# Hash attention and a SwiGLU block on one core: which thirds of x are transposed by DMA, and where one load, one cast of values and one eviction stand

## The chip, the core and the metric

The kernel runs on one core of a Trainium2 chip. Its engines run in parallel, each through its own queue in order: TensorE (PE in the profile; its weight loads are PEld), VectorE (DVE), ScalarE (ACT), GpSimd (POOL) and SyncE (SP), which here only issues DMAs. An instruction that waits holds up everything behind it on the same queue. Time is device microseconds of the core, the median of several runs; lower is better.

## The reference

```python
B, H, S, D = 4, 8, 768, 64                      # d_model = 512, d_ff = 1536
q_bits = (einsum("bhsd,dk->bhsk", q, proj) > 0)  # 6 bits: a bucket per row
k_bits = (einsum("bhsd,dk->bhsk", k, proj) > 0)
mask = q_bucket[..., :, None] == k_bucket[..., None, :]
scores = where(mask, q @ k.T / 8, -1e9)
attn = exp(scores - max); attn = attn / (sum(attn) + 1e-9)
x = (attn @ v), heads side by side               # 3072 x 512
xn = x / sqrt(mean(x * x) + 1e-6) * rms_g
g = xn @ w_gate; silu = g / (1 + exp(-g))
out = (silu * (xn @ w_val)) @ w_out              # 3072 x 512
```

All inputs and the output are float32; the kernel multiplies in fp16 and accumulates in float32.

## The kernel before, in words

**Units.** The work is cut into eight units u of 384 query rows: batch u // 2, half u % 2. For a unit and a head, the scores (transposed, keys on the partitions) come in three chunks of two 128 x 384 matmuls (`scores`, s_ps, L345). The hash bits are extra rows of the stationary and the moving operand, so that a wrong bucket makes the score very negative. ScalarE exponentiates a chunk (`probs`, psb, L357), and TensorE multiplies with the values (`av`, o_ps, L370, 18 matmuls a head), a column of ones giving the sum.

**From heads to x.** Two heads share the one bank of o_ps. VectorE evicts it (`attn_out`: otmp at L384, rcp at L389), which frees the bank for the next pair, and GpSimd multiplies (x at L391, its square sq at L397). `s_step` reduces sq to partial sums of squares (L413). After the last head `norm_scale` (ss at L435, rstd at L439) and `norm` scale the three thirds c of x, 128 rows each, into xn.

**Turning x.** The block needs x with features on the partitions (xnT). There are two ways. `turn_x` makes four 128 x 128 transposes on TensorE (x_ps, L463) and evicts them, on VectorE with one instruction (L469) or on ScalarE with four (L467), multiplying by the gains, a column per block (gcol). `turn_dma` (L427) issues one DMA transpose for the whole third from SyncE; then the gains, as rows (grow), are multiplied in already by the scaling (`scalar_tensor_tensor`, L448). The dictionary ONDMA says how many thirds of a unit go by DMA.

**The block.** For each of 12 slices of 128 hidden features there are four gate and four value matmuls (g_ps, v_ps, L480), a tanh on ScalarE (t, L488) and two instructions on VectorE (a at L497, ht at L498). `project` multiplies with w_out (y_ps, L509), and `store` copies (ysb, L521) and issues the DMA out (L522).

**The order.** It is written out by hand in 192 steps, three per head and unit (two of the first unit and two of the second go first). A step issues the scores of the next chunk, the exponentials of its own, and then whatever `plan[step]` holds, filled by `at(window, step, function)`. Unit u's block runs in the 24 steps in which unit u + 1 attends (NS = 24): `norm` at step 4 of them, the DMA transposes at step 5, and by `spread` the projection of unit u - 1, the turns on TensorE and the gates, given out evenly over the steps by weights (SCORES, AV, PROJ, FEED, TURN). For a third by DMA a piece of weight TURN without work is kept, except in unit 6. Steps in the list `late` (o_step, s_step, hash and its sends) are appended behind the pieces of `spread`, so that on VectorE an eviction stands behind the a and ht of the same step; the exceptions are named in the loop over `order`.

**Pairs of batches 1 to 3.** The table `spots` gives for a pair of heads (b, hp) the step of its load (eight DMAs of 32 x 24 x 32 and one of the values, `load_blocks` and `load_v`), of its transposes on VectorE (`turn_dve`), and of its hash (`hash_one`; the signs, L225, give the bits). `send_bits` issues four DMAs a head from SyncE into the operand; SENDS delays some. `zero_rows` (a memset of 2.65 us on GpSimd) clears the rows behind the bits. `v_prep` casts the values and `v_sum` adds them on GpSimd.

**The end.** After the last head, the projection of unit 6 runs by thirds, with `norm(7)` and the turns of unit 7 in it; then come unit 7's gates and its projection.

The PSUM banks of x_ps, g_ps, v_ps, y_ps and the like are three, used in turn; s_ps has two buffers, xnT two, xn one, ysb three. A DMA from SyncE waits for the one eight issues before it.

Of the kernel before, what the change touches and what calls it, by code (L numbers as in the profile page):

```python
# [19 lines left out]
DMODEL = H * D  # L20
DFF = 1536
NF = DFF // 128
# [11 lines left out]
def kernel(  # L34
# [12 lines left out]
    nc = tc.nc  # L47
# [27 lines left out]
    grow = const.tile([128, DMODEL], FP32, name="grow")  # L75
# [8 lines left out]
    def bank(name, shape=None, dt=FP32):  # L84
        return gps.tile(shape or [128, 512], dt, name=name, tag="g")
# [326 lines left out]
    def sumsq(u, hp, sq):  # L412
        nc.vector.tensor_reduce(  # L413
            out=ssp[u % 2][:, hp, :], in_=sq, op=ALU.add, axis=AX.X
        )
# [3 lines left out]

    rstds = {}  # L420

    ONDMA = {2: 2, 3: 2, 4: 2, 5: 2, 6: 3}

    def turn_dma(u, c):
        if c == 0:
            xnT[u] = npool.tile([128, 4, HALF], FP16, name="xnT", bufs=2)
        nc.sync.dma_start_transpose(  # L427
            out=xnT[u][:, :, c * 128 : (c + 1) * 128], in_=xn[u][:, c, :]
        )


    def norm_scale(u):

        ss = spool.tile([128, 3], FP32, name="ss")
        nc.vector.tensor_reduce(  # L435
            out=ss, in_=ssp[u % 2].rearrange("p h c -> p c h"), op=ALU.add, axis=AX.X
        )
        rstd = spool.tile([128, 3], FP32, name="rstd")
        nc.gpsimd.tensor_tensor(out=rstd, in0=ss, in1=mhalf, op=ALU.pow)  # L439
        rstds[u] = rstd  # L440

    def norm(u):
        if u not in rstds:
            norm_scale(u)
        xn[u] = npool.tile([128, 3, DMODEL], FP16, name="xn")
        for c in range(3 if u else 2):
            if c < ONDMA.get(u, 0):
                nc.vector.scalar_tensor_tensor(  # L448
                    out=xn[u][:, c, :], in0=x[u][:, c, :], scalar=rstds[u][:, c : c + 1],
                    in1=grow, op0=ALU.mult, op1=ALU.mult,  # L450
                )
            else:
                norm_third(u, c, nc.vector.tensor_scalar_mul)

    def norm_third(u, c, mul):
        mul(xn[u][:, c, :], x[u][:, c, :], rstds[u][:, c : c + 1])

    def turn_x(u, c, act=False):
        if c == 0:
            xnT[u] = npool.tile([128, 4, HALF], FP16, name="xnT", bufs=2)  # L460
        ps = bank("x_ps", [128, 4, 128], FP16)
        for kt in range(4):
            nc.tensor.transpose(ps[:, kt, :], xn[u][:, c, kt * 128 : (kt + 1) * 128], ident16)  # L463
        dst = xnT[u][:, :, c * 128 : (c + 1) * 128]
        if act:
            for kt in range(4):
                nc.scalar.mul(dst[:, kt], ps[:, kt], gcol[:, kt : kt + 1])  # L467
        else:
            nc.vector.tensor_mul(dst, ps, gcol.unsqueeze(2).to_broadcast([128, 4, 128]))  # L469
# [34 lines left out]
    def project(u, c, f0, f1):  # L504
        if f0 == 0:
            obank[u, c] = bank("y_ps")
        y = obank[u, c]
        for ft in range(f0, f1):
            nc.tensor.matmul(  # L509
                y, ht[u][:, ft, c * 128 : (c + 1) * 128], wo[:, ft, :],  # L510
                start=(ft == 0), stop=(ft == NF - 1),
            )

    def rows_of(u, c):
        b, half = divmod(u, 2)
        rows = out[b * S : (b + 1) * S, :].rearrange("(p c) n -> p c n", c=6)
        return rows[:, 2 * c + half if b in PARITY else 3 * half + c, :]

    def store(u, c):
        ysb = spool.tile([128, DMODEL], FP32, name="ysb", bufs=3)  # L520
        nc.scalar.copy(ysb, obank.pop((u, c)))  # L521
        nc.sync.dma_start(out=rows_of(u, c), in_=ysb)  # L522
# [65 lines left out]
    NS = 24  # L588
# [5 lines left out]
    def at(w, s, f, *a):  # L594
        plan[NS * w + s].append(lambda: f(*a))
# [70 lines left out]
    at(0, 1, load_natural, nc.sync, 0, 3, "q")  # L666
    at(0, 2, load_v, nc.sync, 0, 2)
    at(0, 2, load_v, nc.sync, 0, 3)
    at(0, 60, nc.sync.dma_start, grow, moe_rms_g.partition_broadcast(128))
    at(0, 65, nc.scalar.mul, grow, grow, float(DMODEL) ** 0.5)  # L670
    at(0, 6, v_prep, 0, 1)
    at(0, 15, v_prep, 0, 2)
    at(0, 19, v_prep, 0, 3, nc.vector)
# [9 lines left out]
    for hp, ts in ((0, (8, 22, 23, 24, 25, 24, 39, 26, 28, 42)), (1, (20, 27, 28, 29, 30, 29, 41, 32, 33, 43))):  # L683
# [15 lines left out]
    spots = {  # L699
        (1, 2): (34, (48, 48), (46, 46), 51),  # L700
        (1, 3): (45, (55, 56), (57, 58), 61),
        (2, 0): (50, (63, 64, 65, 66), (67, 69, 70, 71), 73),
        (2, 1): (62, (72, 73, 75, 81), (82, 83, 84, 85), 86),
        (2, 2): (70, (87, 88, 89, 90), (91, 93, 94, 95), 97),
        (2, 3): (84, (96, 97, 99, 105), (105, 106, 106, 107), 108),
# [2 lines left out]
        (3, 2): (114, (135, 136, 137, 139), (140, 141, 142, 143), 145),  # L708
        (3, 3): (132, (144, 145, 147, 153), (153, 154, 154, 155), 156),
    }  # L710
    for i, t in ((0, 39), (1, 41), (2, 57), (3, 61)):
        at(0, t, zero_rows, i)
    TX = 37

# [6 lines left out]
    def s_step(u, hp):  # L721
# [3 lines left out]
        else:  # L725
            sumsq(u, hp, sq)

    late = []
    for n, (u, h) in enumerate(order):
        t = 3 * n + 4 - ((u, h) == (0, H - 1))  # L730
        for part in range(2):
            at(0, t + part, av, u, h, part)
        if h % 2:
            if (u, h) == (0, H - 1):

                at(0, t + 1, o_step, u, h // 2, nc.vector)
                at(0, t + 1, norm_scale, u)
                at(0, t + 1, nc.vector.tensor_scalar_mul, gcol, gcol, float(DMODEL) ** 0.5)
                at(0, t + 2, hash_only, 1, 1)
                at(0, t + 2, hash_signs, 1, 1)  # L740
                at(0, t + 2, norm, u)
                at(0, TX-1, norm_third, u, 2, nc.scalar.mul)
                at(0, TX + 1, send_pair, 1, 1)
                for c in range(3):
                    at(0, TX, turn_x, u, c, c == 2)
                continue
            if (u, h) == order[-1]:
                at(0, t + 1, o_step, u, h // 2, nc.vector)
                continue

            steps = [(t + 1, o_step), (t + (6 if h < 7 else 3), s_step)]
            for s, step in steps:
                if s < 2 * NS or s % NS in (2, 4):
                    at(0, s, step, u, h // 2)
                else:
                    late.append((s, step, u, h // 2))
# [20 lines left out]
            inserts[2 * b * NS + s] = (MEAN, v_mean, b, hp, 4)  # L777


    SENDS = {(2, 0, 0): 77, (2, 0, 1): 77, (2, 2, 1): 101, (3, 2, 1): 149}  # L780

    def place(t, step):
        at(0, t, *step)
        if step[0] is hash_one:
            late.append((t, hash_bits, *step[1:]))
            for hh in range(2):
                s = SENDS.get((*step[1:], hh), t)
                late.append((max(s, t), send_bits, *step[1:], hh))
# [26 lines left out]
    for u in range(7):  # L815
        gates = [
            (FEED, f is gate and part == 0, [(0, f, u, ft, part)])
            for ft in range(NF) for f in (gate, value) for part in range(2)
        ]
        if u == 0:  # L820
            t0 = TX + 1
            spread(t0, 2 * NS - t0, gates)
            continue
        t0 = NS * (u + 1)
        at(0, t0 + 4, norm, u)
        for c in range(ONDMA.get(u, 0)):
            at(0, t0 + 5, turn_dma, u, c)
        pieces = []
        for i in range(9):
            c, n = divmod(i, 3)  # L830
            steps = [(0, project, u - 1, c, 4 * n, 4 * n + 4)]
            if n == 2:
                steps.append((1, store, u - 1, c))
            pieces.append((4 * PROJ, True, steps))
            if i in (6, 7):
                thirds = ((0,), (1, 2))[i - 6]
                for c in thirds:
                    if c >= ONDMA.get(u, 0):
                        pieces.append((TURN, False, [(0, turn_x, u, c)]))
                    elif u < 6:  # L840
                        pieces.append((TURN, False, []))
        lag, after = LAGS[u - 1 : u + 1]
        spread(t0 + lag, NS + after - lag, pieces + gates)
# [6 lines left out]
    def behind_norm(t):  # L850

        return t - t % NS + 9 if 1 <= t % NS < 9 else t

    for (b, hp), (load, kturns, qturns, _) in spots.items():
        at(0, load, load_blocks, nc.sync, b, hp)
        at(0, load, load_v, nc.sync, b, hp)
        at(0, min(kturns + qturns), new_pair, b, hp)
        for w, turns in (("k", kturns), ("q", qturns)):
            for i, t in enumerate(turns):
                at(0, t, turn_dve, b, hp, w, i, len(turns))  # L860
            t = turns[-1] + 1
            at(0, t if (b, hp) == (1, 2) else behind_norm(t), cast_pool, b, hp, w)
        t = 54 if (b, hp) == (1, 2) else behind_norm(qturns[-1] + 2)
        at(0, t, v_prep, b, hp)
        at(0, t, v_sum, b, hp)

# [13 lines left out]
    for t in range(LAST, LAST + 6):  # L880
        for f in plan[t]:
            f()
    for c in range(2):
        project(6, c, 0, NF)
        store(6, c)
    norm(7)
    project(6, 2, 0, 4)
    for c, f0, f1 in ((0, 4, 6), (1, 6, 8), (2, 8, NF)):
        turn_x(7, c, c == 1)
        project(6, 2, f0, f1)  # L890
    store(6, 2)
    for ft in range(NF):
# [37 lines left out]
```

## Time and profile before

| | |
|---|---|
| time, median of 3 runs | 328.9 us (328.4 to 329.17) |
| the profiled execution's own time | 328.83 us |
| its span | 326.7 us, 7791 instructions |
| granted TensorE clock | 1.000 |
| unit 1's first gate (g_ps) | at 79.27 us |
| unit 6's first gate | at 268.16 us |
| unit 7's first gate | at 300.08 us |
| DMA transposes (L427) | 11, SyncE busy 1.20 to 2.01 us in each |
| transposes on TensorE (L463) | 52 |

The table is to be read against TensorE's timeline: a gate of a unit is the first instruction that needs the whole of xnT, so its start shows whether the turning of x came in time. Times are from the span's start.

### The profile page before, as it was taken

The numbers are of one execution on the slowest core, as the hardware profiler recorded it, in microseconds if no ns is written. First come the engines' busy times: TensorE is split into PE (matmuls) and PEld (weight loads), VectorE is DVE, ScalarE is ACT, GpSimd is POOL, SyncE is SP. The second block draws the span as 40 slices with busy tenths as digits, with TensorE's granted clock in tenths as the row PEclk, the third lists the DMA queues.
The fourth block names the chain that finished last, engine by engine and source line by source line (L and its number), as shares of the span: only waits on it lengthen the run. The fifth ranks groups of instructions, "written<-read, shape, count | busy, mean of one in ns | idle before, by whom it ended". The sixth has DMA issues, their size and how long they took to land.

```text
span 326.7 us, 7791 instructions
## 1 busy us (share of the span) xinstructions
PE 321.3 (98%) x2955; PEld 194.1 (59%) x2955; DVE 231.2 (71%) x515; ACT 228.3 (70%) x332; POOL 157.6 (48%) x204
## 2 busy tenths in 40 slices
PE   8999999999999999999999999999999999999996
PEld 3576666656565565655566565655666556665554
DVE  5887876859888559874888568885766536675870
ACT  6999887667688667776777677787777767744322
POOL 3999759955974363731873521752682220221000
PEclk9999999999999999999999999999999999999999
DMA  7952999989328828343547047002100040002002
GB/s 216 353 163 69 230 216 200 181 138 182 102 39 155 152 79 154 54 98 99 91 102 141 9 138 135 7 1 69 68 5 3 7 127 14 2 2 90 8 2 96
DMA packets 85741, 32.63 MB, mean 100 GB/s; under 512 B 70908, under 2 KB 82632, under 8 KB 85704
## 3 DMA queue, kind: packets, MB, share of 16 engines
q1 hardware_dynamic: 81800, 27.35, 36.1%
q0 software_dynamic: 3680, 4.72, 8.6%
q8 instruction: 23, 0.38, 0.5%
q14 instruction: 14, 0.11, 0.1%
q10 hardware_dynamic: 224, 0.07, 0.1%
HBM read 28.58 MB, written 6.29 MB: 107 GB/s over the span
## 4 chain that ended last, share of the span: by engine, by line
PE 95%; DMA 2%; ACT 1%; SPq 1%; issue 0%
PE s_ps L345 20%; PE g_ps L480 19%; PE v_ps L480 19%; PE y_ps L509 17%; PE o_ps L370 11%; PE d_ps L216 2%; PE t_ps L156 2%; PE d_ps L236 2%; DMA qn<-in_q_dram 1%; PE x_ps L463 1%; ACT psb L357 1%; PE y_ps L528 1%; DMA xnT<-xn 1%; PE m_ps L329 1%; PE z_ps L576 1%; SPq L427 0%
## 5 line engine op out<-in xcount | busy, mean ns | idle before, releaser
L357 ACT ACTIVATE psb<-s_ps,ebias 128x768 f16<-128x768 f32 x192 | 168.1, 901 | 21.2 <-PE s_ps L345 20.4
L345 PE MATMUL s_ps<-QK 128*128 128x384 f16 (+1 forms) x384 | 93.5, 326 | 1.3 <-ACT psb L357 1.1
L488 ACT ACTIVATE t<-g_ps 128x384 f32<-128x384 f32 x96 | 47.3, 492 | 51.9 <-PE g_ps L480 50.2
L480 PE MATMUL g_ps<-xnT,wg 128*128 128x384 f16 x384 | 82.5, 326 | 0.2 <-DMA xnT<-xn 0.2
L480 PE MATMUL v_ps<-xnT,wv 128*128 128x384 f16 x384 | 81.8, 326 | 0.0
L497 DVE SCALAR_TENSOR_TENSOR a<-t,g_ps 128x384 f32<-128x384 f32 x96 | 53.0, 552 | 28.8 <-ACT t L488 27.3
L391 POOL TENSOR_TENSOR x<-otmp,rcp 128x384 f32<-128x384 f32 x30 | 25.1, 837 | 97.8 <-DVE rcp L389 97.6
L509 PE MATMUL y_ps<-wo,ht 128*128 128x512 f16 x276 | 67.9, 379 | 0.0
L498 DVE SCALAR_TENSOR_TENSOR ht<-a,v_ps 128x384 f16<-128x384 f32 x96 | 53.2, 554 | 12.1 <-PE v_ps L480 4.1
L370 PEld LDWEIGHTS <-psb 128*128 128x128 f16 x1152 | 51.8, 97 | 16.1 <-issue 1.2
L370 PE MATMUL o_ps<-vl,psb 128*128 128x65 f16 x1152 | 55.8, 193 | 0.1
L345 PEld LDWEIGHTS <-QK 128*128 128x128 f16 (+1 forms) x384 | 34.8, 98 | 34.9 <-issue 9.3
L480 PEld LDWEIGHTS <-wg 128*128 128x128 f16 x384 | 35.1, 97 | 21.8 <-issue 0.6
L480 PEld LDWEIGHTS <-wv 128*128 128x128 f16 x384 | 35.1, 97 | 20.7 <-issue 0.2
L509 PEld LDWEIGHTS <-ht 128*128 128x128 f16 x276 | 24.8, 98 | 22.8
L521 ACT COPY ysb<-y_ps 128x512 f32<-128x512 f32 x23 | 13.5, 587 | 17.5 <-PE y_ps L509 17.5
L384 DVE TENSOR_TENSOR otmp<-o_ps,cvb 128x390 f32<-128x390 f32 x32 | 17.9, 558 | 9.8 <-PE o_ps L370 9.8
L208 POOL CAST QK<-qT 64x768 f16<-64x768 f32 x20 | 16.5, 823 | 10.4 <-DVE qT L195 9.5
L397 POOL TENSOR_TENSOR sq<-x 128x384 f32<-128x384 f32 x24 | 19.9, 827 | 1.9
L208 POOL CAST QK<-kT 64x768 f16<-64x768 f32 x20 | 16.4, 822 | 4.6 <-DVE kT L195 2.5
L195 DVE STREAM_TRANSPOSE kT<-kL 128x192 f32<-128x192 f32 x32 | 16.5, 521 | 0.0
L195 DVE STREAM_TRANSPOSE qT<-qL 128x192 f32<-128x192 f32 x32 | 16.3, 526 | 0.0
(85 smaller groups left out, 267.5 us busy)
## 6 DMA issues: line engine op xcount, KB each, us to landing
vn<-in_v_dram SPq DMA_DIRECT2D x16, 384.0 KB
out_dram<-ysb SPq DMA_DIRECT2D x23, 256.0 KB
qL<-in_q_dram SPq DMA_DIRECT2D x40, 96.0 KB
kL<-in_k_dram SPq DMA_DIRECT2D x40, 96.0 KB
kn<-in_k_dram SPq DMA_DIRECT2D x5, 384.0 KB
qn<-in_q_dram SPq DMA_DIRECT2D x5, 384.0 KB
wg<-in_moe_w_gate_dram POOLq DMA_DIRECT2D x2, 768.0 KB, 9.5
wv<-in_moe_w_val_dram POOLq DMA_DIRECT2D x2, 768.0 KB, 11.9
```

Source lines behind the costliest of these rows:

```text
L195: nc.vector.transpose(dst.rearrange("p (c t r) -> p r c t", c=6, r=4)[:, r], src.rearrange("p (r c) d -> p r c d", r=4)[:, r],)
L208: nc.gpsimd.tensor_copy(QK[b, 2 * hp + hh, "h"][0:64, o : o + S], src[64 * hh : 64 * hh + 64, :])
L345: nc.tensor.matmul(ps[:, j, 0:HALF], QK[b, h, "h"][rows, S + jt * 128 : S + (jt + 1) * 128], QK[b, h, "h"][rows, half * HALF : (half + 1) ...
L357: nc.scalar.activation(psb[u, h][:, 2 * ch : 2 * ch + 2, :], sps.pop((u, i))[:, :, 0:HALF], AF.Exp, bias=ebias, scale=ESCALE,)
L370: nc.tensor.matmul(o[:, c, hh, 0:65], psb[u, h][:, jt, c * 128 : (c + 1) * 128], vls[b % 2][:, h, 2 * (jt % 3) + jt // 3 if b in PARITY el ...
L391: eng.tensor_mul(xd.rearrange("p c (h d) -> p c h d", h=2), tmp[:, :, :, 0:64], r.to_broadcast([128, 3, 2, 64]),)
L397: eng.tensor_mul(sq, xd, xd)
L480: nc.tensor.matmul(ps, w[:, kt, fs], xnT[u][:, kt, :], start=(kt == 0), stop=(kt == 3))
L488: nc.scalar.activation(t, fbank[u, ft, "g_ps"], AF.Tanh, scale=0.5)
L497: nc.vector.scalar_tensor_tensor(out=a, in0=t, scalar=1.0, in1=g, op0=ALU.add, op1=ALU.mult)
L498: nc.vector.scalar_tensor_tensor(out=ht[u][:, ft, :], in0=a, scalar=0.5, in1=vv, op0=ALU.mult, op1=ALU.mult)
L509: nc.tensor.matmul(y, ht[u][:, ft, c * 128 : (c + 1) * 128], wo[:, ft, :], start=(ft == 0), stop=(ft == NF - 1),)
```

## The change

- Unit 1 turns two thirds of x by DMA (before: none), unit 6 two (before: three), unit 7 one (before: none).
- The gains as rows (grow) are loaded at step 24 (before 60) and multiplied at step 49 (before 65), so that they are there for unit 1.
- The load of pair (2,0) goes from step 50 to 54, the bits of (1,2)'s second head from 51 to 54, its `v_prep` and `v_sum` from 54 to 57, and the memset of the fourth operand from 61 to 69.
- AHEAD: the eviction (otmp) of unit 6's second pair stands ahead of the pieces of its step and not behind them.
- In unit 7 the reductions of the partial squares come two steps sooner. At the end, `norm(7)` comes after the first third's projection; its third third is scaled by ScalarE; the first third is turned by DMA, the second by VectorE's eviction and the third by ScalarE's, four y_ps matmuls behind each turn.

```diff
--- before.py
+++ after.py
@@ -419,7 +419,7 @@
 
     rstds = {}
 
-    ONDMA = {2: 2, 3: 2, 4: 2, 5: 2, 6: 3}
+    ONDMA = {1: 2, 2: 2, 3: 2, 4: 2, 5: 2, 6: 2, 7: 1}
 
     def turn_dma(u, c):
         if c == 0:
@@ -443,7 +443,7 @@
         if u not in rstds:
             norm_scale(u)
         xn[u] = npool.tile([128, 3, DMODEL], FP16, name="xn")
-        for c in range(3 if u else 2):
+        for c in range(3 if 0 < u < 7 else 2):
             if c < ONDMA.get(u, 0):
                 nc.vector.scalar_tensor_tensor(
                     out=xn[u][:, c, :], in0=x[u][:, c, :], scalar=rstds[u][:, c : c + 1],
@@ -666,8 +666,8 @@
     at(0, 1, load_natural, nc.sync, 0, 3, "q")
     at(0, 2, load_v, nc.sync, 0, 2)
     at(0, 2, load_v, nc.sync, 0, 3)
-    at(0, 60, nc.sync.dma_start, grow, moe_rms_g.partition_broadcast(128))
-    at(0, 65, nc.scalar.mul, grow, grow, float(DMODEL) ** 0.5)
+    at(0, 24, nc.sync.dma_start, grow, moe_rms_g.partition_broadcast(128))
+    at(0, 49, nc.scalar.mul, grow, grow, float(DMODEL) ** 0.5)
     at(0, 6, v_prep, 0, 1)
     at(0, 15, v_prep, 0, 2)
     at(0, 19, v_prep, 0, 3, nc.vector)
@@ -699,7 +699,7 @@
     spots = {
         (1, 2): (34, (48, 48), (46, 46), 51),
         (1, 3): (45, (55, 56), (57, 58), 61),
-        (2, 0): (50, (63, 64, 65, 66), (67, 69, 70, 71), 73),
+        (2, 0): (54, (63, 64, 65, 66), (67, 69, 70, 71), 73),
         (2, 1): (62, (72, 73, 75, 81), (82, 83, 84, 85), 86),
         (2, 2): (70, (87, 88, 89, 90), (91, 93, 94, 95), 97),
         (2, 3): (84, (96, 97, 99, 105), (105, 106, 106, 107), 108),
@@ -708,7 +708,7 @@
         (3, 2): (114, (135, 136, 137, 139), (140, 141, 142, 143), 145),
         (3, 3): (132, (144, 145, 147, 153), (153, 154, 154, 155), 156),
     }
-    for i, t in ((0, 39), (1, 41), (2, 57), (3, 61)):
+    for i, t in ((0, 39), (1, 41), (2, 57), (3, 69)):
         at(0, t, zero_rows, i)
     TX = 37
 
@@ -725,6 +725,8 @@
         else:
             sumsq(u, hp, sq)
 
+
+    AHEAD = {(6, 1)}
     late = []
     for n, (u, h) in enumerate(order):
         t = 3 * n + 4 - ((u, h) == (0, H - 1))
@@ -748,9 +750,9 @@
                 at(0, t + 1, o_step, u, h // 2, nc.vector)
                 continue
 
-            steps = [(t + 1, o_step), (t + (6 if h < 7 else 3), s_step)]
+            steps = [(t + 1, o_step), (t + (3 if h == 7 else 4 if u == 7 else 6), s_step)]
             for s, step in steps:
-                if s < 2 * NS or s % NS in (2, 4):
+                if s < 2 * NS or s % NS in (2, 4) or (step is o_step and (u, h // 2) in AHEAD):
                     at(0, s, step, u, h // 2)
                 else:
                     late.append((s, step, u, h // 2))
@@ -777,7 +779,7 @@
             inserts[2 * b * NS + s] = (MEAN, v_mean, b, hp, 4)
 
 
-    SENDS = {(2, 0, 0): 77, (2, 0, 1): 77, (2, 2, 1): 101, (3, 2, 1): 149}
+    SENDS = {(1, 2, 1): 54, (2, 0, 0): 77, (2, 0, 1): 77, (2, 2, 1): 101, (3, 2, 1): 149}
 
     def place(t, step):
         at(0, t, *step)
@@ -860,7 +862,7 @@
                 at(0, t, turn_dve, b, hp, w, i, len(turns))
             t = turns[-1] + 1
             at(0, t if (b, hp) == (1, 2) else behind_norm(t), cast_pool, b, hp, w)
-        t = 54 if (b, hp) == (1, 2) else behind_norm(qturns[-1] + 2)
+        t = 57 if (b, hp) == (1, 2) else behind_norm(qturns[-1] + 2)
         at(0, t, v_prep, b, hp)
         at(0, t, v_sum, b, hp)
 
@@ -880,13 +882,16 @@
     for t in range(LAST, LAST + 6):
         for f in plan[t]:
             f()
-    for c in range(2):
-        project(6, c, 0, NF)
-        store(6, c)
+    project(6, 0, 0, NF)
+    store(6, 0)
     norm(7)
+    norm_third(7, 2, nc.scalar.mul)
+    turn_dma(7, 0)
+    project(6, 1, 0, NF)
+    store(6, 1)
     project(6, 2, 0, 4)
-    for c, f0, f1 in ((0, 4, 6), (1, 6, 8), (2, 8, NF)):
-        turn_x(7, c, c == 1)
+    for c, f0, f1 in ((1, 4, 8), (2, 8, NF)):
+        turn_x(7, c, c == 2)
         project(6, 2, f0, f1)
     store(6, 2)
     for ft in range(NF):
```

## The prediction

> **What bounds the kernel now.** I read the page first, for the engines' busy times.
>
> ```profile
> PE 321.3 (98%) x2955; PEld 194.1 (59%) x2955; DVE 231.2 (71%) x515; ACT 228.3 (70%) x332; POOL 157.6 (48%) x204
> ```
>
> TensorE is busy 98% of the span and no other engine is above 71%. A change can win only by taking instructions off TensorE or by closing one of its few holes, and it loses where it opens one. So I walked TensorE's timeline for places where a matmul starts later than the one before it allows. (Back to back, in these rows, an s_ps, g_ps or v_ps matmul takes 0.163 us, a y_ps one 0.216, an x_ps transpose 0.056, since 12 of them fill 0.67 us of the chain.) After step 48 of the plan four such places lie near the edited lines.
>
> The chain of waits, at the first gate of unit 6 (start, us, what):
>
> ```profile
> 262.97 0.88 PE y_ps L509 x4
> ...
> 264.27 1.22 SPq L427
> ...
> 265.58 2.45 DMA xnT<-xn
> ...
> 268.16 0.81 PE g_ps L480 x4
> ```
>
> The third DMA transpose of unit 6 is issued at 265.58 and the gate can start only at 268.16, 2.58 us later. The s_ps pair before it is through at 267.46 + 0.33 = 267.79, so 0.38 us is lost.
>
> TensorE's timeline at two more places (start, us, engine, line):
>
> ```profile
> 241.07 0.49 PE L345 MATMUL s_ps<-QK 128*128 128x384 f16 x2
> 241.68 0.43 PE L370 MATMUL o_ps<-vl,psb 128*128 128x65 f16 x9
> ...
> 271.31 0.81 PE L480 MATMUL v_ps<-xnT,wv 128*128 128x384 f16 x4
> 272.25 0.48 PE L345 MATMUL s_ps<-QK 128*128 128x384 f16 x2
> ```
>
> At 241.07 two s_ps matmuls need 0.33 us, and o_ps starts 0.61 later: 0.28 lost. At 271.31 four v_ps matmuls need 0.65, and s_ps starts 0.94 later: 0.29 lost. VectorE's and ScalarE's timelines say why:
>
> ```profile
> 239.84 0.56 DVE L497 SCALAR_TENSOR_TENSOR a<-t,g_ps 128x384 f32<-128x384 f32 x1 [1.24 <-ACT t L488]
> 240.50 0.56 DVE L498 SCALAR_TENSOR_TENSOR ht<-a,v_ps 128x384 f16<-128x384 f32 x1
> 240.97 0.56 DVE L384 TENSOR_TENSOR otmp<-o_ps,cvb 128x390 f32<-128x390 f32 x1
> ...
> 270.91 0.49 ACT L488 ACTIVATE t<-g_ps 128x384 f32<-128x384 f32 x1 [0.61 <-PE g_ps L480]
> 271.30 1.69 ACT L357 ACTIVATE psb<-s_ps,ebias 128x768 f16<-128x768 f32 x2
> ```
>
> The single o_ps bank is freed by otmp, which is queued behind an `a` that waits 1.24 us for ScalarE. And the exponential at 271.30, whose s_ps buffer TensorE wants back, is queued behind a `t` that waits for gate 1.
>
> Last the SyncE queue in the stage of unit 1:
>
> ```profile
> 71.30 0.39 SPq L522 DMA_DIRECT2D out_dram<-ysb  x1
> 71.79 3.34 SPq L120 DMA_DIRECT2D qL<-in_q_dram  x4
> 75.23 2.65 SPq L120 DMA_DIRECT2D kL<-in_k_dram  x4
> 77.98 0.58 SPq L106 DMA_DIRECT2D vn<-in_v_dram  x1
> 78.66 5.74 SPq L304 DMA_DIRECT2D QK<-bits  x8
> ```
>
> From 71.79 to 78.56 it issues the load of pair (2,0). A transpose put here unaided would wait for it.
>
> **The change part by part.** Sums are made against the profiled execution's 328.83 us (span 326.7 and 2.1 around it), 0.07 under the 328.9 median.
>
> *Unit 1.* TensorE loses 8 transposes, 8 x 0.056 = 0.45 us. The eight at 77.22 now occupy 0.58 (s_ps follows at 77.80), 0.13 over their pitch, because x is scaled late: three scalings took 2.77 us, and that hole closes too. TensorE alone would reach unit 1's first gate at 79.27 - 0.58 = 78.69. The gate also waits for the DMA. The new SyncE order is: store 71.30, four sends of pair (1,2)'s first head, two transposes, a store, the other four sends, then the load of (2,0). The sends wait for `bits` on VectorE (71.44 to 72.00) and cost 5.74/8 = 0.72 each: 72.05 to 74.95. x's first third is ready earlier, by rstd at 73.80 plus 0.75 (a scaling with grow takes 748 ns). So the first transpose is issued at 75.0 and the second 1.34 later (a pair takes 2.56, its last 1.22). With 2.58 from the last issue to the gate the gate starts at 78.95: gain 0.3. Bounds: a gain of 0.58 if the landing is hidden; a loss of 1.0 if both transposes take the 2.01 us issue of the slowest one on record (second issue 77.1, and 0.6 more to the gate, 80.3). I take 0.3, since unit 4 repeats the 2.58: its second transpose is issued at 190.23 and its gate starts at 192.81.
>
> *What moves with it.* The (2,0) load is issued about 9.3 us later, 81.1 to 87.9; its first kT transpose on VectorE is at 90.91, about 90.4 afterwards. The last kL issue starts near 85.9; with the 2.58 us that a transpose needs from issue to use its data is there at 88.5, two microseconds ahead. What is queued next on SyncE, the bits of pair (1,3), is issued at 88.62 now; SyncE is through with the load and a store by about 88.3, and the s_ps that wants these bits is at 92.4: nothing. VectorE's two scalings with grow cost 0.75 instead of 0.48 and two 0.69 turns go: VectorE is ahead. The load of grow goes from 85.41 to SyncE's gap before 34.79, 256 KB in a stretch of 316 GB/s, 0.8 us of transfer. Queued beside it is the first wv load, issued at 33.39, landing 10.6 us later at 43.99, first used at 45.3: 1.3 of cover, cost nothing (bounds 0 and 0.3). Its multiplication, 0.64 us, goes to ScalarE near 67.7, before a wait of 1.10 for y_ps: nothing. The memset of 2.65 us and the values of (1,2) swap order on GpSimd; the casts of pair (1,3)'s first head, wanted by 92, end near 90.6 instead of 87.6: nothing, with 1.4 us of cover.
>
> *Unit 6.* One third goes back to TensorE: +0.22. The gate then waits for the second transpose only, which lands 1.3 us sooner, so the 0.38 goes. The turned third comes from VectorE 1.1 us after its x_ps starts, and TensorE fills 1.42 (x_ps 0.22, y_ps 0.86, s_ps 0.33). What is late next is otmp, now behind that 0.69 us turn: done near 268.3, wanted at 269.3. One more weight in the spreading also moves gate 1 by half a gate, so the waiting `t` comes after the next exponential and not ahead of it; I count the 0.29 as won. Together -0.45 (bounds 0, if the 0.29 hole only moves to another step and a new 0.2 opens, and -0.6).
>
> *One otmp sooner.* VectorE is idle for the 1.24 us before 239.84, and o_ps of that pair is done near 238.8. Ahead of the waiting `a`, otmp ends by 239.8: -0.28 (bounds 0 and -0.28).
>
> *Unit 7.* TensorE loses 4 transposes, -0.22, and the last turn is no longer VectorE's 0.69 us, which held the gate by 0.09 (300.08, where 299.13 + 0.86 = 299.99 was free). The last turn becomes ScalarE's four pieces, each waited for by its own matmul: about +0.05. The DMA third: the reduction of heads 4 and 5 moves ahead, so otmp starts near 292.2, not 292.67, x's first third is scaled by 296.3, the transpose is issued there, behind the store of 294.95, and usable 2.6 later at 298.9, a microsecond before the gate at 299.8. Two stores now stand behind it on SyncE for 1.2 us; only ysb's third buffer could feel that, and it isn't wanted before unit 7's own stores: nothing. The scaling that ScalarE takes over (0.73) fits between the copies at 294.9 and 296.9. Net -0.25 (bounds -0.3 and +0.5, the latter if the transpose is a microsecond and a half late).
>
> Sum: -0.3 - 0.45 - 0.28 - 0.25 = -1.28, so 328.83 - 1.28 = 327.55, and 327.6 on the scale of the median.
>
> **The rivals.** *The transposes of unit 1 land late.* Every 0.1 us on SyncE's side is 0.1 of TensorE idle. For it: the first transpose of unit 6 was 2.01 us in issue, and 71 to 75 us still moves 199 GB/s. Against it: the other ten rows take 1.20 to 1.33, and the load that filled the engines from 74 to 81 is now behind. With two issues of 2.0 the gate comes at 80.3, unit 1 turns from -0.3 to +1.0, and the time is 328.9: no change.
>
> The Trainium skill speaks for this rival: its page "VectorE: DVE Perf Modes", section "Rules for kernel authors", advises TensorE for a 128x128 transpose wherever a PSUM destination is acceptable and the DMA crossbar only otherwise. The same page's section "The three transpose paths" gives 390 ns against 1309 ns, which for a third of four blocks would be an estimated 5.2 us by DMA. The trace differs: a third takes 2.45 us from issue to landing here, and 0.22 on TensorE.
>
> *The holes of units 6 and 7 only move.* In-order queues may give the 0.29 and half of unit 7's gain back at another step: 327.6 + 0.5 = 328.1, or 328.4 with otmp's too.
>
> *The late load blocks VectorE (slower).* A kT transpose of (2,0) whose data has not landed stops VectorE's queue, and with it the gates' banks. It decides once kL is usable later than about 91.5, and pays 1:1 from there. For it: the load of (1,2) was 11.10 us in qL and 8.89 in kL when the weights streamed. At such rates kL would be there at 81.1 + 20.0 + 2 = 103 and the time 327.6 + 11.5 = 339; at the 4.71 and 2.67 of (1,3) it is there near 90.5 and free; halfway between, near 96.8, the time is 333. Against it: from 81 to 90 the engines moved only 95 GB/s, so nothing competes.
>
> **How the numbers follow.** Forecast, 327.2 to 328.1: 0.62. Transposes late, 328.2 to 329.0: 0.15. Holes that move, 328.0 to 328.6: 0.13. Late load, above 329.5: 0.10. Predicted 327.6. The range 327.1 to 329.0 takes in the first three and leaves out the last. 0.2% is 0.66 us, about what separates a change of this kernel from none. Faster than 328.24 are the forecast and some of the second and third cases: 0.70; within 0.2% 0.19; slower 0.11.
>
> **What would show it.** Unit 1's first gate near 78.9, with a short wait on DMA xnT; SyncE issuing transposes at 75.0 and 76.3. No hole before o_ps near 241 nor before s_ps near 272; unit 6's first gate waiting on nothing. Unit 7's first gate about 1.3 us ahead of 300.08, with no DMA wait. I am wrong if the DMA wait in unit 1 is over 1 us, if VectorE idles for DMA at kT near 90, or if PE waits for ScalarE or VectorE appear where none were.

## The result and the profile after

The changed kernel takes 329.81 us (median of 11 runs, 328.84 to 330.65), beside 328.74 for the kernel before on the same chip (11 runs, 327.74 to 329.23). The ratio is 1.0032, with a 95% interval of 1.0022 to 1.0043: slower by about 1.1 us. The prediction said 327.6, in a range of 327.1 to 329.0, and gave slower 11%. It was wrong.

The profiled execution took 330.44 us, 1.6 more than the one of before. Its page has the engines nearly as they were (TensorE's busy time is the same to 0.1 us, with eight matmuls fewer in the program):

```profile
PE 321.3 (98%) x2946; PEld 194.1 (59%) x2947; DVE 228.6 (70%) x512; ACT 228.2 (69%) x333; POOL 157.0 (48%) x204
```

A busy time that stays while there is less work doesn't say that nothing was won: records of matmuls overlap, a few are missing, and holes of a few tenths hide in it. So TensorE's timeline is read again. Three waits are in it that the kernel before does not have (start, us, engine, line, what; in brackets the idle time and what ended it):

```profile
45.41 0.81 PE L480 MATMUL g_ps<-xnT,wg 128*128 128x384 f16 x4
47.02 0.82 PE L480 MATMUL v_ps<-xnT,wv 128*128 128x384 f16 x4 [0.80 <-DMA wv<-in_moe_w_val_dram]
...
79.41 1.02 PE L509 MATMUL y_ps<-wo,ht 128*128 128x512 f16 x4
81.11 0.48 PE L480 MATMUL g_ps<-xnT,wg 128*128 128x384 f16 x2 [0.67 <-DVE rcp L389]
...
93.76 0.49 PE L480 MATMUL g_ps<-xnT,wg 128*128 128x384 f16 x2
94.88 0.48 PE L345 MATMUL s_ps<-QK 128*128 128x384 f16 x2 [0.64 <-DMA QK<-bits]
```

The same three places in the kernel before:

```profile
44.79 0.81 PE L480 MATMUL g_ps<-xnT,wg 128*128 128x384 f16 x4
45.44 0.81 PE L480 MATMUL v_ps<-xnT,wv 128*128 128x384 f16 x4
...
78.40 1.03 PE L509 MATMUL y_ps<-wo,ht 128*128 128x512 f16 x4
79.27 0.49 PE L480 MATMUL g_ps<-xnT,wg 128*128 128x384 f16 x2
...
91.92 0.49 PE L480 MATMUL g_ps<-xnT,wg 128*128 128x384 f16 x2
92.37 0.48 PE L345 MATMUL s_ps<-QK 128*128 128x384 f16 x2
```

Measured from start to start, less the pitch of the matmuls between, the holes are 0.96 us (45.41 + 0.65 = 46.06, and the values start at 47.02), 0.83 and 0.80. In the kernel before, the first two did not exist (78.40 + 0.86 = 79.26 at the second place), and at the third there was 0.12. The name "DVE rcp" at the second is a coincidence of two ends: that instruction ended within 0.01 us of the gate's start, but the last DMA transpose was issued at 78.55, and 78.55 + 2.56 = 81.11. Gates that the profile does put down to DMA xnT start as long after their last issue: 2.58 us in the kernel before (unit 6), 2.57 and 2.56 in two runs below.

SyncE's timeline shows how the last two came about:

```profile
73.05 0.40 SPq L106 DMA_DIRECT2D vn<-in_v_dram  x1
73.55 0.40 SPq L522 DMA_DIRECT2D out_dram<-ysb  x1
74.06 2.95 SPq L304 DMA_DIRECT2D QK<-bits  x4
77.11 2.63 SPq L427 DMA_TRANSPOSE xnT<-xn  x2
79.84 0.54 SPq L522 DMA_DIRECT2D out_dram<-ysb  x1
80.44 2.86 SPq L304 DMA_DIRECT2D QK<-bits  x4
83.40 3.52 SPq L120 DMA_DIRECT2D qL<-in_q_dram  x4
87.02 2.65 SPq L120 DMA_DIRECT2D kL<-in_k_dram  x4
89.72 0.64 SPq L106 DMA_DIRECT2D vn<-in_v_dram  x1
90.47 0.40 SPq L522 DMA_DIRECT2D out_dram<-ysb  x1
90.97 5.99 SPq L304 DMA_DIRECT2D QK<-bits  x8
```

From 73 on it is never free. The transposes leave at 77.11 (forecast 75.0), the bits of pair (1,3), ready on VectorE at 90.44, at 90.97 and behind a load of values.

The gains of the end came. TensorE's timeline at the first gate of unit 6 has no wait:

```profile
269.07 1.03 PE L509 MATMUL y_ps<-wo,ht 128*128 128x512 f16 x4
269.94 0.49 PE L345 MATMUL s_ps<-QK 128*128 128x384 f16 x2
270.26 0.81 PE L480 MATMUL g_ps<-xnT,wg 128*128 128x384 f16 x4
```

The table gives the distance between the first gates of the units, against the kernel before (us). "End" is from the last matmul's start to the end of the span.

| kernel | 0 to 1 | 1 to 2 | 2 to 5 | 5 to 6 | 6 to 7 | 7 to last matmul | end |
|---|---|---|---|---|---|---|---|
| changed | +1.22 | +0.67 | +0.01 | -0.43 | -0.59 | +0.04 | 3.38 (before 3.01) |
| grow at 17 | -0.09 | +0.96 | +0.03 | -0.43 | -0.59 | +0.04 | 3.38 |
| grow alone | +0.59 | +0.53 | +0.01 | -0.04 | 0.00 | -0.02 | 3.01 |
| units 6, 7 alone | +0.01 | -0.01 | -0.03 | -0.43 | -0.59 | +0.04 | 3.02 |
| unit 1 alone | +1.34 | +0.89 | +0.01 | +0.40 | 0.00 | -0.01 | 3.39 |
| values of (2,0) later | +0.24 | -0.01 | +0.09 | -0.43 | -0.59 | +0.04 | 3.38 |
| one third in unit 1 | -0.35 | -0.01 | +0.06 | -0.43 | -0.59 | +0.04 | 3.48 |
| bits behind transposes | -0.57 | +1.70 | 0.00 | -0.43 | -0.59 | +0.03 | 3.39 |
| other rows | +0.02 | +0.03 | +0.03 | +0.08 | 0.00 | -0.02 | 3.45 |
| bits by GpSimd | -0.58 | 0.00 | -0.02 | -0.43 | -0.59 | +0.05 | 3.14 |
| the same, two DMAs more | -0.57 | 0.00 | -0.02 | -0.43 | -0.59 | +0.05 | 3.02 |
| two DMAs more alone | 0.00 | +0.17 | +0.02 | -0.23 | 0.00 | -0.02 | 3.40 |

For the changed kernel the row adds up to +0.93 (each figure is rounded), and +0.37 at the end makes +1.30. The spans differ by 1.92 (328.62 against 326.70); the rest of that lies before unit 0's first gate, at 45.41 here and 44.79 before. That gate lies between 44.62 and 45.41 in the profiles of this study; the two kernels below that have the same program up to there as the changed one have it at 44.84 and 44.87, and one that has the same as the kernel before has it at 45.13. Two others that share their program up to there (grow at 17, values of (2,0) later) differ by 0.71. So it varies by as much from run to run, and the 0.62 is not put down to the change.

### The profile page after: what moved, and what is told of

Its sections match the earlier page's. It is cut to its first block, busy times and chain, and to the rows that moved or that the text cites. A ratio compares the mean times of both kernels' runs of the same rounds, so it can differ in the third digit from the quotient of the medians.

```text
span 328.6 us, 7774 instructions
## 1 busy us (share of the span) xinstructions
PE 321.3 (98%) x2946; PEld 194.1 (59%) x2947; DVE 228.6 (70%) x512; ACT 228.2 (69%) x333; POOL 157.0 (48%) x204
## 4 chain that ended last, share of the span: by engine, by line
PE 88%; DMA 6%; DVE 2%; POOL 2%; ACT 1%; issue 0%; SPq 0%; POOLq 0%
PE v_ps L480 19%; PE g_ps L480 18%; PE s_ps L345 17%; PE y_ps L509 17%; PE o_ps L370 9%; DMA wv<-in_moe_w_val_dram 4%; PE d_ps L216 2%; PE t_ps L156 2%; PE d_ps L236 1%; PE z_ps L576 1%; DMA QK<-bits 1%; PE y_ps L528 1%; DMA xnT<-xn 1%; ACT psb L357 1%; POOL QK L178 0%; PE x_ps L463 0%
## 5 line engine op out<-in xcount | busy, mean ns | idle before, releaser
L469 DVE TENSOR_TENSOR xnT<-x_ps,gcol 128x512 f16<-128x512 f16 x9 | 6.1, 690 | 16.4 <-PE x_ps L463 16.4
```

## The experiments

Ratios are against the kernel before, run on the same chip, with 95% intervals.

**Grow loaded into an idle stretch.** In the changed kernel:

```diff
-    at(0, 24, nc.sync.dma_start, grow, moe_rms_g.partition_broadcast(128))
+    at(0, 17, nc.sync.dma_start, grow, moe_rms_g.partition_broadcast(128))
```

> Edit: the changed kernel with the load of grow at step 17 in place of step 24, into a stretch (26 to 30 us) in which the DMA engines move nearly nothing; all else as changed. Theory W (the load of grow ahead of the weights makes the first value weights late, 13.0 us after their issue and not 10.6): the hole of 0.96 us before the first v_ps of unit 0 goes to 0.1 or less, the first wv load lands about 10.6 us after its issue, the issue of pair (1,2)'s qL takes about 11 us again and not 12.7, the bits of (1,2) go out 0.4 us sooner and the hole at unit 1's first gate falls from 0.83 to about 0.4, that at the s_ps of pair (1,3) from 0.80 to 0.3 or 0.5. Time about 328.1, 1.7 under the changed kernel and 0.6 under the one before. Rival (the landing of the weights only varies between runs, grow has no part in it): the hole stays near 1 us and the time near 329.8.

Measured: 329.01 us, ratio 1.0007 (0.9996 to 1.0018). The first hole is gone; the first wv load lands 10.5 us after its issue (13.0 in the changed kernel, 10.6 before). Unit 1's times are near the forecast: transposes at 75.01 and 76.43 (forecast 75.0 and 76.3), gate at 79.00 (78.95). Counted from unit 0's first gate, which is 0.17 sooner here than in the kernel before, the gain is 0.09, though, and not the 0.3 of the prediction: TensorE still waits 0.48 for the transposes there. And only half of the 1.7 us came back, since the third hole did not shrink, it grew to 1.09. The profile puts that wait down to DMA QK<-bits: TensorE reached that s_ps sooner, and the bits did not land sooner. They were ready at 88.33 and left SyncE at 88.69 (88.62 in the kernel before), but their first packet moved 2.15 us after that (90.84), and not 1.33 (89.95).

**Grow alone**, in the kernel before:

```diff
-    at(0, 60, nc.sync.dma_start, grow, moe_rms_g.partition_broadcast(128))
-    at(0, 65, nc.scalar.mul, grow, grow, float(DMODEL) ** 0.5)
+    at(0, 24, nc.sync.dma_start, grow, moe_rms_g.partition_broadcast(128))
+    at(0, 49, nc.scalar.mul, grow, grow, float(DMODEL) ** 0.5)
```

> Edit: the kernel before with nothing but the load of grow at step 24 (60) and its multiplication at step 49 (65). Theory W: a hole of 0.8 to 1.0 us opens before the first v_ps of unit 0, the load of (1,2) on SyncE ends 2 us later, nothing else changes: 329.6 to 329.8, 0.9 to 1.1 above the kernel before. Rival: no hole, 328.7, the same as before.

Measured: 330.09 us, ratio 1.0035 (1.0022 to 1.0049), 1.2 above. The hole at the first v_ps is there, 0.58 us in the profiled run, less than the 0.8 to 1.0 expected. "Nothing else changes" was wrong: SyncE is through with the load of (1,2), which competes with the weights, later, the loads behind it follow later, and the bits of (1,2) come late to their s_ps at 83.99, for 0.54. A load of 256 KB is felt a second time fifty microseconds on.

**The end alone**: the changed kernel with the parts of unit 1 taken back.

```diff
-    ONDMA = {1: 2, 2: 2, 3: 2, 4: 2, 5: 2, 6: 2, 7: 1}
+    ONDMA = {2: 2, 3: 2, 4: 2, 5: 2, 6: 2, 7: 1}
...
-    at(0, 24, nc.sync.dma_start, grow, moe_rms_g.partition_broadcast(128))
+    at(0, 60, nc.sync.dma_start, grow, moe_rms_g.partition_broadcast(128))
...
-        (2, 0): (54, (63, 64, 65, 66), (67, 69, 70, 71), 73),
+        (2, 0): (50, (63, 64, 65, 66), (67, 69, 70, 71), 73),
...
```

> Edit: the changed kernel with all parts that belong to unit 1 taken back (two thirds by DMA, grow, the load of (2,0), the memset, the sends and values of (1,2)); units 6 and 7 and the otmp as changed. If the gains of the end stand by themselves, as read between the gates of units 5 and 7 (0.43 + 0.59 us), the time is 327.7, 1.0 under the kernel before, and units 0 to 5 are as before to 0.1 us. Rival (they only take up slack that the late start left): 328.4 or more.

Measured: 327.83 us, ratio 0.9973 (0.9962 to 0.9984), 1.04 under the kernel before; -0.43 and -0.59 between the gates and nothing elsewhere. The gain of this part is real and independent.

**Unit 1 alone**: the kernel before with the other half.

```diff
-    ONDMA = {2: 2, 3: 2, 4: 2, 5: 2, 6: 3}
+    ONDMA = {1: 2, 2: 2, 3: 2, 4: 2, 5: 2, 6: 3}
...
```

> Edit: the kernel before with only the parts that belong to unit 1. The three holes read in the changed kernel (0.96 at the first v_ps, 0.25 net at unit 1's gate, 0.68 net at the s_ps of pair (1,3)) add up to 1.9: 330.6, and all of it is there by the first gate of unit 2. Rival (the losses are elsewhere, or depend on the end): 329.7 or less.

Measured: 331.69 us, ratio 1.0095 (1.0075 to 1.0114), 2.8 above. The three holes are there, the first larger (1.38) and the third too (1.02). Two DMAs more cost 0.38 at the end, as in the changed kernel. And not all was over by unit 2, as had been expected: unit 6, which in this kernel still turns three thirds by DMA, has its gate 0.40 later. Its transposes fell on the pair loads and took 3.5 and 3.2 us from issue to last packet, where 1.97 is usual. The changed kernel had the same slow pair (3.66 and 3.38), and with two thirds it cost nothing.

**Values later.** With grow at 17, and

```diff
-        at(0, load, load_v, nc.sync, b, hp)
+        at(0, 66 if (b, hp) == (2, 0) else load, load_v, nc.sync, b, hp)
```

> Edit: the changed kernel with the load of grow at step 17 (as in the run before it) and the values of pair (2,0) loaded at step 66, apart from its blocks (54). In the run with grow at 17 the bits of pair (1,3) left SyncE at 88.69 and their first packets moved at 90.5, behind the 1536-byte packets of those values; s_ps waited 1.09 us. Theory Q (the small sends stand behind a large load in the DMA queue itself, beyond SyncE's own lateness): with that load gone the bits go out at 88.3, when they are ready, the first packets follow within 1 us, and the hole falls from 1.09 to 0.2 or less; time about 328.0, 1.0 under the run with grow at 17 alone. Rival (only SyncE's late issue counts): the bits were ready at 88.33, so 0.36 of the hole goes and 0.7 stays; 328.65.

Measured: 327.78 us, ratio 0.9975 (0.9963 to 0.9988). The third hole is gone to the 0.12 of before. The bits now leave SyncE 0.03 us after VectorE has them (ready at 89.37, issued at 89.40), against 0.36 in the run before, and their first packet follows 1.40 us after the issue, against 2.15. So the late issue, 0.33, was the smaller part, and the queue of the DMA engines, 0.75, the larger. What the Trainium skill says in "DMA: Bandwidth & Descriptors", section "Queues, rings and completion order", that on each DMA engine descriptors of a queue are consumed in ring order, agrees with this: in the run before, the values were issued ahead of the bits, their last packet ended at 91.36 and the bits began at 90.84. The trace doesn't name the DMA engine of a packet, so that they stood behind one another on the same engines is argued and not shown. (The profiled execution of this run took 328.81 us, 1.0 above the run's median, so its row in the table may hold more than a usual execution.)

**One third in unit 1**, with the edits so far:

```diff
-    ONDMA = {1: 2, 2: 2, 3: 2, 4: 2, 5: 2, 6: 2, 7: 1}
+    ONDMA = {1: 1, 2: 2, 3: 2, 4: 2, 5: 2, 6: 2, 7: 1}
```

> Edit: the run with the values of (2,0) at step 66, and in unit 1 one third of x by DMA where the change has two. Its gate then waits for one transpose, issued near 75.0 and usable near 77.6, over a microsecond early: the DMA wait of 0.3 to 0.48 us at unit 1's gate goes, and 4 transposes come back to TensorE, +0.22. Theory (unit 1's gate is held by the second transpose, 2.57 us after its issue): 0.1 to 0.25 under the run with two thirds, no DMA wait before the first g_ps of unit 1, about 327.85. Rival (the gate is held by VectorE, which does the turn of the third third, a kT transpose and an otmp before it): the wait stays, with VectorE's name, and the time is 0.2 above the run with two thirds.

Measured: 328.14 us, ratio 0.9981 (0.9971 to 0.9990). In the profile the wait at unit 1's gate is gone, TensorE waits for nothing from 40 to 120 us, so VectorE did not hold that gate. The theory had the time 0.1 to 0.25 under the run with two thirds (327.78); it is not under it, and the intervals overlap: as a matter of time the comparison is inconclusive. The end, 3.48 and so 0.10 later with one DMA less, takes back part of what the gate wins.

**Bits behind the transposes**, with two thirds again:

```diff
-    SENDS = {(1, 2, 1): 54, (2, 0, 0): 77, (2, 0, 1): 77, (2, 2, 1): 101, (3, 2, 1): 149}
+    SENDS = {(1, 2, 0): 53, (1, 2, 1): 54, (2, 0, 0): 77, (2, 0, 1): 77, (2, 2, 1): 101, (3, 2, 1): 149}
```

> Edit: the run with the values of (2,0) at step 66, and the four sends of pair (1,2)'s first head behind the two DMA transposes of unit 1 and not ahead of them. Theory (SyncE's 2.95 us of sends stand between the scaled x and its transposes): the transposes are issued near 74.4 and 75.8, the gate is free by 78.4, the hole of 0.48 at unit 1's gate goes, and the sends end near 80.0, in time for the s_ps that wants them near 82.6; about 327.65. Rival (x's scaled thirds are what the transposes wait for, and the sends cost nothing): gate as before, and the bits of (1,2) may come late: 328.0 or more.

Measured: 328.90 us, ratio 1.0005 (0.9990 to 1.0019). Unit 1's gate is 0.57 sooner, as expected, and the bits of (1,2) come in time. But SyncE then waits idle for the scaled x, from 71.96 to 74.78, and begins the load of (2,0) 1.9 us later than in the run without this edit (both counted from unit 0's first gate): the bits of (1,3) leave at 90.16, their s_ps waits 1.49, and unit 2's gate another 0.33. VectorE now waits for the late load as well, 0.72 us at the first kT of (2,0). The queue was only paid at another place.

**Other rows.** In the kernel before, as many bytes as grow has, ahead of the weights, from 128 different rows:

```diff
+    at(0, 24, nc.sync.dma_start, grow, moe_w_out[0:128, :])
     at(0, 60, nc.sync.dma_start, grow, moe_rms_g.partition_broadcast(128))
```

> Edit: the kernel before, with one more load of 128 x 2 KB into grow at step 24, from 128 different rows of w_out; the load and the multiplication of grow stay at 60 and 65, so nothing that is computed changes. Ahead of the weights stand as many bytes as in the run with grow at step 24 alone, whose 128 packets all read the same 2 KB, took 0.13 to 0.21 us each (not 0.085) and left the DMA engines 45% idle from 34 to 36 us. Theory R (it is the reading of one row by 128 packets that makes the load slow): the load takes about 0.8 us at full rate, the first wv load lands about 11.5 us after its issue, within its cover: no hole at the first v_ps, time 328.9 as before. Rival B (256 KB of any kind ahead of the weights delay them by two microseconds): a hole of 0.6 to 1.4 us at the first v_ps, 329.6 to 330.1.

The windows of the trace (us; then busy time of PE, PEld, DVE, ACT and POOL, the clock, the DMA engines' share, GB/s) from 34 to 36 us: first the kernel before,

```profile
34.00:36.00 2.00, 2.00 (x29) 1.70 (x26) 1.97 (x6) 1.56 (x2) 0.53 (x2) 1.00 1.11 210
```

then grow alone,

```profile
34.00:36.00 2.00, 2.00 (x31) 1.75 (x28) 1.97 (x6) 1.49 (x2) 0.53 (x2) 1.00 0.59 157
```

and other rows:

```profile
34.00:36.00 2.00, 2.00 (x29) 1.70 (x26) 1.97 (x7) 1.59 (x2) 0.53 (x2) 1.00 1.12 308
```

In this stretch the engines move 308 GB/s in all with 128 rows ahead, and 157, with 41% idle, with one row. The load's own packets say the same: from 128 rows all but the last two start within 1.5 us, from one row the 128 take 4.2 us (34.53 to 38.74). The first wv load lands after 11.2 us, against 12.6 with grow (12.6 to 13.4 in the three kernels with one row ahead of the weights, 10.1 to 11.9 in the nine with nothing ahead), and there is no hole at the first v_ps. That is theory R, as far as one run with another tensor as the source can show it. The time, 329.46 us with a ratio of 1.0022 (1.0011 to 1.0034), lies between the two theories all the same: the profile has +0.14 up to the last matmul, and 0.44 more behind it, which neither theory had priced. The last two experiments are about that end.

**Bits by GpSimd.** With grow at 17, the values of (2,0) at 66, and two thirds in unit 1:

```diff
-    SENDS = {(1, 2, 1): 54, (2, 0, 0): 77, (2, 0, 1): 77, (2, 2, 1): 101, (3, 2, 1): 149}
+    SENDS = {(1, 2, 0): 53, (1, 2, 1): 54, (2, 0, 0): 77, (2, 0, 1): 77, (2, 2, 1): 101, (3, 2, 1): 149}
...
     def send_bits(b, hp, hh):
+        eng = nc.gpsimd if (b, hp, hh) == (1, 2, 0) else nc.sync
...
-            nc.sync.dma_start(
+            eng.dma_start(
```

> Edit: the run with the values of (2,0) at step 66, and the four sends of pair (1,2)'s first head issued by GpSimd at step 53 (it is idle from 74.3 to 80.2) and not by SyncE ahead of the transposes. With the sends moved behind the transposes on SyncE's own queue, unit 1's gate came 0.57 us sooner, and everything behind them on SyncE 1.8 us later, for which the s_ps of pair (1,3) waited 1.49. Theory (SyncE's queue from 72 to 91 is full; it is the sum of its issues that decides): with four issues taken off it the transposes leave near 74.5, unit 1's gate is 0.5 to 0.6 sooner than in the kernel before, the bits of (1,3) leave when they are ready, no hole there; with 0.98 of units 6 and 7, 327.3. Rival (GpSimd's sends land later than SyncE's or hold up x for pair 0 of unit 2, L391): a wait at the s_ps of pair (1,2) near 82 or at o_ps, 328 or more.

Measured: 327.40 us, ratio 0.9951 (0.9931 to 0.9970): the lowest median of all, under both kernels, though its interval overlaps those of the end alone and of the next run. In the profiles the gates add up to -1.57, against -1.00 for the end alone, so unit 1's part is worth 0.57 there once its queues are in order. SyncE's timeline in that run (lines stand one further down in its code):

```profile
74.67 2.63 SPq L428 DMA_TRANSPOSE xnT<-xn  x2
77.39 0.53 SPq L523 DMA_DIRECT2D out_dram<-ysb  x1
78.02 2.96 SPq L305 DMA_DIRECT2D QK<-bits  x4
...
88.10 5.25 SPq L305 DMA_DIRECT2D QK<-bits  x7
```

and GpSimd's (from 73.82 it issues the four sends):

```profile
72.97 0.88 POOL L440 TENSOR_TENSOR rstd<-ss,mhalf 128x3 f32<-128x3 f32 x1 [1.71 <-DVE ss L436]
73.82 2.12 POOL L305 DMA_DIRECT2D QK<-bits  x4
79.72 0.83 POOL L392 TENSOR_TENSOR x<-otmp,rcp 128x384 f32<-128x384 f32 x1 [3.78 <-DVE rcp L390]
```

The gate of unit 1 starts at 78.74, the bits of (1,3) leave when they are ready, and TensorE waits for no DMA between 60 and 120 us. The Trainium skill's "DMA: Bandwidth & Descriptors", section "Issuing engines are not separate DMA queues", says that another issuing engine saves only the time to initiate, usually small beside the DMA. The mechanism agrees; here that time, four issues of 0.74 us, stood ahead of transposes that a gate waits for, and it was not small.

**The count of DMAs.** The run above with two DMAs more (the values of (1,0) and (1,1) by heads):

```diff
-        eng.dma_start(
-            out=vn.rearrange("p h c d -> p h (c d)"),
-            in_=v[b, 2 * hp : 2 * hp + 2].rearrange("h (p c) d -> p h (c d)", c=6),
-        )
+        n = 1 if (b, hp) in ((1, 0), (1, 1)) else 2
+        for h in range(0, 2, n):
+            eng.dma_start(
+                out=vn[:, h : h + n].rearrange("p h c d -> p h (c d)"),
+                in_=v[b, 2 * hp + h : 2 * hp + h + n].rearrange("h (p c) d -> p h (c d)", c=6),
+            )
```

> Edit: the run with sends by GpSimd, and the values of pairs (1,0) and (1,1) loaded a head at a time, two DMAs more at a place where SyncE is idle. At the end of the program SyncE waits for eight DMA semaphores in a fixed order, 0.063 us a wait; DMAs take them in turn. In the kernel before the last DMA has the last of the eight and the program ends 3.01 us after the last matmul's start; with one DMA more it has the first and the end comes at 3.46 to 3.48; with two more, the second, 3.38. Theory E (the number of DMAs modulo eight sets up to 0.44 us at the end): the run with four sends taken from SyncE ends near 3.14, this one at 3.01, 0.1 sooner. Rival (the end varies for another reason): no such order.

and the same edit in the kernel before:

> Edit: the kernel before with the values of pairs (1,0) and (1,1) loaded a head at a time: two DMAs more (as many as the change adds), nothing else. Theory E: all gates as before within 0.1 us of each other's distances, the end 3.38 us after the last matmul's start and not 3.01, time 329.1, 0.37 above the kernel before. Rival: the end at 3.01, time 328.75, the same as before.

Measured: the first 327.63 us, 0.9958 (0.9938 to 0.9977), with its end at 3.02 as theory E has it; the 0.1 us can't be told in the time. The second 329.42 us, 1.0019 (1.0004 to 1.0033), with its end at 3.40, 0.39 later than before: two loads cut in halves in an idle stretch cost the kernel before about 0.2%. That all gates stay within 0.1 us failed: one distance is 0.17 longer and one 0.23 shorter, for a reason that no run here shows. SyncE's last instructions (us after the last matmul's start, and the semaphore waited for) show why the end is later. The last DMA's semaphore is 109 in the kernel before and 103 in the changed one, both are there at 2.12, and the waits behind it in the fixed order are still to be made:

```
before    0.35 103   0.42 104   0.49 105   0.55 106   1.04 107   1.46 108   2.12 109   2.18 drain
changed   1.47 100   2.12 103   2.18 104   2.25 105   2.31 106   2.37 107   2.43 108   2.49 109   2.56 drain
```

## Why the prediction was wrong, point by point

- **"The load of grow ... cost nothing (bounds 0 and 0.3)" failed**, and it is the largest of the failed terms: 0.96 us at the first v_ps, 0.58 and 1.38 in the two kernels with the same load at that place, and by way of SyncE's late loads 0.5 more further on. The step was right in its form (0.8 us of transfer against 1.3 of cover) and wrong in the size: the 0.8 came from a rate of 316 GB/s that other loads had. A broadcast whose 128 packets read one row took longer, even alone: in the run with grow at 17 its packets run from 25.43 to 27.24, 1.81 us. The kernel before showed it already. There grow is issued at 85.41 behind two stores of 256 KB each; these two windows lines are the stretch of the stores and, taking the packets in the order of their issue, that of grow:

```profile
85.40:86.80 1.40, 1.40 (x18) 0.90 (x16) 0.97 (x2) 1.06 (x3) 1.28 (x3) 1.00 0.99 360
86.80:89.00 2.20, 2.20 (x25) 1.04 (x24) 2.02 (x5) 1.14 (x2) 2.08 (x3) 1.00 0.50 128
```

  The stores go through at 360 GB/s with the engines full, the broadcast takes 2.2 us with the engines half idle. A term of 2.2 us in place of 0.8 would have eaten the cover of 1.3, and 0.3 was no honest upper end. Beside the weights it took longer still, 4.2 us, and the first wv load landed 2.4 us later after its issue than before (13.0, and not 10.6). The cover was 1.5 (45.44 less 43.96), which leaves 0.9 of the 0.96.
- **"The late (2,0) load: nothing" failed.** 0.67 us at the s_ps of (1,3). The prediction asked when SyncE is through (88.3 by its count) and did not ask what the DMA engines still had in their queue then. With SyncE within 0.1 us of its time in the kernel before, in the run with grow at 17, the loss was 0.96. The rival that the load blocks VectorE's kT did not happen in the changed kernel; the price was paid one queue further.
- **"Unit 1: -0.3" failed in the changed kernel** (about +0.25: the 1.22 between the gates, less 0.96), because the step took SyncE's times from a trace in which the loads were early. Its law, gate 2.58 us behind the last issue, held wherever the gate waited for a transpose (2.56, 2.57, 2.56 and 2.57 at unit 1's gate). With grow out of the way the gate stood within 0.05 us of its forecast, but in part by luck, since unit 0's first gate came 0.17 sooner: the term itself was -0.09 there, and +0.24 in the run with the values later, whose program is the same up to that gate. It came out in full, at -0.57 and -0.58, only with the four sends out of the transposes' way, and without a loss elsewhere only with them off SyncE. The rival "transposes late" was right in its direction, but by SyncE's lateness: both issues were short (1.33 and 1.20). The estimate of 5.2 us that the prediction drew from the Trainium skill's page "VectorE: DVE Perf Modes", section "The three transpose paths", is far from the 2.0 us that a third takes here from issue to last packet.
- **Not in the sum at all:** two DMAs more, from the two transposes added, +0.37 at the end.
- **The signs named in advance did not come.** The DMA wait at unit 1's gate was 0.83, under the 1 us set, VectorE did not wait for DMA at kT, and no new wait of TensorE for VectorE or ScalarE came but the misnamed one. They watched the rivals thought of; the first v_ps, the s_ps of (1,3) and the end were not among the places.
- **Units 6 and 7 and the otmp held.** Forecast from unit 5's gate to unit 6's: 0.22 - 0.38 - 0.28 = -0.44; measured -0.43 in all eight kernels with this part. From there to unit 7's: -0.29 - 0.25 = -0.54; measured -0.59. The rival "the holes only move" fell.

The prediction's -1.28, with 0.96 + 0.55 + 0.67 + 0.37 for the failed terms, makes +1.27; the profile has +1.30 from unit 0's first gate on, and the medians +1.1. That the sum closes so well is partly due to the way it is made up, since the failed terms are read from that same profile. All failed terms lie in DMA: its queues, and the semaphores at the end. Those that held rest mostly on durations of single instructions, which the trace had.

## What to carry to other kernels

A transfer that is moved has to be costed at three places: the issuing queue, the queue of the DMA engines (what large load is ahead of the small one that somebody waits for), and the transfers beside it, which it delays too. Cover for a load is worth what the worst row of its kind leaves of it; a broadcast is a kind of its own. And where a queue is full, moving an item within it pays at one place what it wins at another, as in the run with bits behind the transposes; taking items off it, onto an engine that is idle, is what closed the holes.

## What was not expected of the hardware

- Reading one 2 KB row by 128 packets is slow: 256 KB in 1.8 us alone, 2.2 us behind two stores, and 4.2 to 5.4 us beside the start of the weights, where the same bytes from 128 rows took 1.5 us but for two packets. Why one row is slow was not tried.
- A send of bits (4.5 KB; those of pair (1,3)) had its first packet 1.32 to 1.47 us after its issue where no load was right ahead, and 2.15 to 2.52 us behind a load of 384 KB (three profiles).
- The end of the program depends on which of the eight semaphores SyncE's last DMA has: 3.01 to 3.02 us after the last matmul's start where it is the last that is waited for (246 DMAs from SyncE, four profiles), 3.14 with two DMAs fewer, 3.45 and 3.48 with one more, 3.38 to 3.40 with two more (six profiles). One wait is 0.063 us.
